# Q, K and V laid out by pairs of heads ahead of the kernel, and rows of decay stored once

## The chip, the cores and the metric

The kernel runs on one core of one Trainium2 chip. The metric is the time on the device in microseconds (us); three runs of the kernel before lay between 1041.75 and 1042.41 us, their median is 1041.98. Engines: TensorE (PE in the profile; PEld its weight loads), VectorE (DVE), ScalarE (ACT), GpSimd (POOL) and SyncE (SP), whose queue issues most transfers.

## The reference

Attention with a decay over 4 batches, 8 heads, 576 positions and 64 columns a head, then two feed-forward layers over 2304 tokens, 512 columns and 2048 inner columns.

```python
scores = scale * np.matmul(q, k.transpose(0, 1, 3, 2))
cum = np.cumsum(np.maximum(s, 0.0), axis=-1)
bias = -(cum[:, :, :, None] - cum[:, :, None, :])
scores = np.where(causal, -1000000000.0, scores + np.minimum(bias, 0.0))
attn = exp(scores - max) / (sum + 1e-09)        # by rows
x = (attn @ v), heads side by side               # 2304 x 512
x = leaky_relu(x @ w_in, 0.01) @ w_out           # first layer
out = softplus(x @ w_in2) @ w_out2               # second layer
```

## The kernel before

The 32 heads are worked off as 16 pairs: head 0 of a pair lies in partitions 0 to 63 of Q and K, head 1 in 64 to 127. A pair is cut into four units of query rows: tile 3 (512 keys), the last 64 rows of both heads together (128 rows), tile 2 (384 keys), and tiles 1 and 0 (256 and 128 keys). Q, K, V, BQ and BK have two buffers each, for even and odd pairs.

Scores of a unit (`Unit.scores`) are two products into one PSUM bank: Q by K in float32, and BQ by BK, which adds the decay. BQ and BK hold a few rows that are not zero: BK has the running sum of s in two parts (rows r and r+1, r = 0 or 64) beside ones in BQ, and BQ has its negative in two parts (rows r+32 and r+33) beside ones in BK. The two parts are a rounded float32r and its rest, since these products are float32r. `decay` scans s into c1 for all 32 heads, writes the four parts into bb, and bb is stored to DRAM (bb_d), from which `rows` fetches a pair's rows in five transfers; pair 0's rows go directly from bb.

Inputs come as they are, by position. `load` reads q and k of a pair into raw tiles (runs of 64 floats a position; in two transfers by head, and the last 64 positions in a third tile, rawl), and v into V. `prep` turns the raw tiles with nine TensorE transposes (line 251 four each for q and k, line 248 one for rawl) into PSUM, and one tick later copies them out: line 256 on ScalarE (Q), line 258 on VectorE (K), lines 260 and 263 on VectorE (the last positions: K and, for each head, Q).

The order of the work is written out by hand: a loop over units in which unit n+1 gets its scores, unit n its maxima (VectorE, line 316) and exponentials (ScalarE, line 330), unit n-1 its divisors and norms (GpSimd, line 341), and unit n-2 its transposes (line 358) and copies. Every engine runs its instructions in that order, so a step that waits holds up all that stands behind it on its engine. `pv` multiplies a pair's attention with V (line 389) one pair later. Each step of the loop may also issue one fill (12 matmuls of the first layer's first group, lines 141 and 586), from the second batch on and once the weights are split (lines 103 to 128). Weights come as 512 KB transfers on SP's queue. `prep(p + 1, ...)` stands at units 0 (q), 2 (last positions) and 1 (k) of pair p, `load(p + 2, ...)` directly behind each, `rows(p + 1)` behind q's at unit 0, `load(p + 1, "v")` at unit 3.

After the attention come the feed-forward layers, with weights streamed in and split on the way.

Of the kernel before, what the change touches and what calls it, by code (L numbers as in the profile page):

```python
# [30 lines left out]
def attn_moe_moe(ctx, tc, q, k, v, s, w1i, w1o, w2i, w2o, out):  # L31
    nc = tc.nc
    B, H, S, D = q.shape
    NT, DM = out.shape
# [21 lines left out]
    xl = keep.tile([P, KD, NT], F32R, tag="xl", name="xl")  # L56
    bb_d = dram.tile([B * H, 2, 2, S], F32R, tag="bb_d", name="bb_d")
    part = dram.tile([2 * B, P, KD, CW], F32, tag="part", name="part")
# [5 lines left out]
    def later(n, fn, *args):  # L64
        todo.setdefault(clock[0] + n, []).append((fn, args))
# [10 lines left out]
    def move(dst, src, queue=nc.sync):  # L76
        queue.dma_start(dst.bitcast(F32), src.bitcast(F32))
# [74 lines left out]
    def decay(cp, first):  # L152

        BH = B * H
        c0 = cp.tile([BH, S], F32, tag="c0", name="c0")
        c1 = cp.tile([BH, S], F32, tag="c1", name="c1")
        bb = cp.tile([BH, 2, 2, S], F32R, tag="bb", name="bb")
        one = bb[:, 0, 0, :].bitcast(F32)
        nc.sync.dma_start(c0, s.rearrange("b h s -> (b h) s"))
        first()  # L160
        nc.vector.memset(one, 1.0)

        nc.vector.tensor_scalar(c0, c0, 0.0, 1.0 / scale, op0=ALU.max, op1=ALU.mult)
        nc.vector.tensor_tensor_scan(c1, one, c0, 0.0, op0=ALU.mult, op1=ALU.add)
        nc.scalar.activation(bb[:, 1, 0, :], c1, AF.Copy)
        nc.scalar.activation(bb[:, 0, 0, :], c1, AF.Copy, scale=-1.0)
        hi = bb[:, 1, 0, :].bitcast(F32)
        nc.vector.tensor_tensor(bb[:, 1, 1, :], c1, hi, op=ALU.subtract)
        nc.vector.tensor_tensor(bb[:, 0, 1, :], hi, c1, op=ALU.subtract)
        return bb  # L170


    def attention(att, ps, fills):
        ident = att.tile([P, P], F32, tag="ident", name="ident")
        make_identity(nc, ident)

# [7 lines left out]
        V = two("V", [P, NB + 1, 2, D])  # L184
        raw = {nm: att.tile([P, NB, 2, D], F32, tag="raw" + nm, name="raw" + nm) for nm in "qk"}
        raw["l"] = att.tile([P, 2, D], F32, tag="rawl", name="rawl")
# [4 lines left out]
        def blank(i):  # L191
            bq, bk = BQ[i].bitcast(F32), BK[i].bitcast(F32)
            nc.gpsimd.memset(bq, 0.0)
            nc.gpsimd.memset(bk, 0.0)
            for j in range(2):
                for c in own[j]:
                    nc.gpsimd.memset(bq[j * D:j * D + 2, c], 1.0)
                nc.gpsimd.memset(bk[j * D + 32:j * D + 34], 1.0)
                nc.gpsimd.memset(Q[i][(1 - j) * D:(2 - j) * D, NB * P + j * TL:NB * P + (j + 1) * TL], 0.0)

        def zeros():
            for i in range(2):
                nc.gpsimd.memset(V[i][TL:, NB, :, :], 0.0)
# [6 lines left out]
        def load(p, nm):  # L210
            if p >= NP:
                return
            b, hs = heads(p)
            src = {"q": q, "k": k, "v": v}.get(nm)
            if nm == "l":
                for x, r in ((q, slice(0, TL)), (k, slice(TL, 2 * TL))):
                    nc.sync.dma_start(raw["l"][r], x[b, hs, NB * P:, :].rearrange("h p d -> p h d"))
                return
            t = V[p % 2] if nm == "v" else raw[nm]
            for j in range(2):  # L220
                nc.sync.dma_start(
                    t[:, :NB, j, :], src[b, hs.start + j, :NB * P, :].rearrange("(c p) d -> p c d", p=P)
                )
            if nm == "v":
                nc.sync.dma_start(t[:TL, NB, :, :], src[b, hs, NB * P:, :].rearrange("h p d -> p h d"))

        def rows(p, src, queue=(nc.sync, nc.sync)):

            if p < NP:
                b, hs = heads(p)  # L230
                for j in range(2):
                    h, r = b * H + hs.start + j, j * D
                    of = lambda e, c: src[h, e, :, c] if src is bb_d else src[h:h + 1, e, :, c]
                    n = 0
                    for c in own[j]:
                        m = n + c.stop - c.start
                        move(BQ[p % 2][r + 32:r + 34, c], of(0, slice(n, m)), queue[j])
                        n = m
                    move(BK[p % 2][r:r + 2], of(1, slice(0, S)), queue[j])

        def prep(p, nm):

            if p >= NP:
                return
            tag, bufs = ("a", 1) if p or nm == "q" else ("m", 1) if nm == "k" else ("t", 2)
            pm = ps.tile([P, 512], F32, tag=tag, name="pt_qk", bufs=bufs)
            if nm == "l":
                nc.tensor.transpose(pm[:, :P], raw[nm].rearrange("p h d -> p (h d)"), ident)
            else:
                for c in range(NB):  # L250
                    nc.tensor.transpose(pm[:, c * P:(c + 1) * P], raw[nm][:, c].rearrange("p h d -> p (h d)"), ident)  # L251

            def out():
                qt, kt = Q[p % 2], K[p % 2]
                if nm == "q" or nm == "k" and not p:
                    nc.scalar.activation((qt if nm == "q" else kt)[:, :NB * P], pm, AF.Copy)
                elif nm == "k":
                    nc.vector.tensor_copy(kt[:, :NB * P], pm)
                else:
                    nc.vector.tensor_copy(kt[:, NB * P:], pm[:, TL:2 * TL])  # L260
                    for j in range(2):
                        r = slice(j * D, (j + 1) * D)
                        nc.vector.tensor_copy(qt[r, NB * P + j * TL:NB * P + (j + 1) * TL], pm[r, :TL])

            later(1, out)


        class Unit:
# [11 lines left out]
            def scores(self):  # L280
                i = self.p % 2
                self.ps = [ps.tile([P, 512], F32, tag=f"s{j}", name="pt_s", bufs=2) for j in range(2)]
                if self.last:

                    for j, pt in enumerate(self.ps):
                        for x, y in ((Q[i], K[i]), (BQ[i], BK[i])):
                            nc.tensor.matmul(  # L287
                                pt[:, :self.W], x[:, NB * P:], y[:, j * self.W:(j + 1) * self.W],
                                start=x is Q[i], stop=x is BQ[i],
                            )  # L290
                    return

                for t, c in self.subs:
                    for x, y in ((Q[i], K[i]), (BQ[i], BK[i])):
                        for j in range(2):
                            r = slice(j * D, (j + 1) * D)
                            nc.tensor.matmul(  # L297
                                self.ps[j][:, c], x[r, t * P:(t + 1) * P], y[r, :(t + 1) * P],
                                start=x is Q[i], stop=x is BQ[i],
                            )  # L300
# [122 lines left out]
        def first():  # L423
            for nm in "qkl":
                load(0, nm)

        with pool("cum", side="right") as cp:
            bb = decay(cp, first)
            blank(0)
            for nm in "qkl":  # L430
                prep(0, nm)
                tick()
            tick()
            rows(0, bb, (nc.sync, nc.scalar))
            masks()
            zeros()
            blank(1)
            load(1, "q")
            load(0, "v")
            move(bb_d, bb)  # L440
            load(1, "k")
            load(1, "l")
        fill = fills()
# [10 lines left out]
        for n in range(len(units) + 3):  # L454
# [13 lines left out]
            if i == 0:  # L468
                prep(p + 1, "q")
                load(p + 2, "q")  # L470
                rows(p + 1, bb_d)
            elif i == 2:
                prep(p + 1, "l")
                load(p + 2, "l")
            tick()
# [8 lines left out]
            if u2:  # L484
                u2.evacuate(0)
                u2.transpose(1)
            if i == 1:
                prep(p + 1, "k")
                load(p + 2, "k")
            elif i == 3 and p + 1 < NP:  # L490
                load(p + 1, "v")
            elif i in (0, 2) and p:
                pv(p - 1, i == 0)
# [257 lines left out]


# [18 lines left out]
```

## Time and profile before

| | |
|---|---|
| median of three runs | 1041.98 us |
| profiled execution, whole | 1041.97 us |
| its span, first to last instruction | 1040.2 us |
| TensorE busy | 1009.9 us (97%), 5632 matmuls |
| VectorE, ScalarE, GpSimd busy | 512.5, 545.1, 581.3 us |
| moved by DMA | 61.20 MB in 89070 packets, 59616 of them under 512 B |
| granted clock | 0.995 |

The attention stage runs to about 280 us, and the feed-forward layers take the rest. Busy shares over the whole span say little of the stages; the stretches below do. Matmuls are pipelined, so the busy time of one reaches under the start of the next.

### The profile page before, as it was taken

To read this page: it belongs to the slowest core of one execution; us is meant where nothing else is said; L and a number is where in the kernel's file an instruction comes from. 1 tells how busy PE (TensorE), PEld (TensorE's weight loads), DVE (VectorE), ACT (ScalarE), POOL (GpSimd) and SP (SyncE) were. 2 spreads that over 40 slices of the span, in tenths; PEclk is the share of its full clock that TensorE was granted. 3 is DMA by queue.
4 is the path that set the end of the run, shared out by engine and by line. 5 is a ranking of instruction groups with operands and counts; after the bars stand their busy time and mean duration, and the time that the engine had idled before them with its cause. 6 is when DMAs were issued, how large, how long until landed. Compare 5 with 4: busy or idle time off the path is not lost.

```text
span 1040.2 us, 15671 instructions
## 1 busy us (share of the span) xinstructions
PE 1009.9 (97%) x5632; PEld 829.6 (80%) x5632; DVE 512.5 (49%) x1174; ACT 545.1 (52%) x1170; POOL 581.3 (56%) x592
## 2 busy tenths in 40 slices
PE   7899999999999999999999998999999999999998
PEld 4668788888898888888888886888777887788886
DVE  5886756555202222222232245645675677567443
ACT  4776767665436333333344354676556545564452
POOL 5765544543327433643456667666866676667453
PEclk9999999999999999999999999999999999999999
DMA  6433433231053101210121021001200121010202
GB/s 146 126 86 79 106 89 99 73 77 37 24 183 119 41 1 41 81 41 1 49 74 41 1 80 42 25 17 41 81 27 15 41 82 37 5 40 21 82 21 81
DMA packets 89070, 61.20 MB, mean 59 GB/s; under 512 B 59616, under 2 KB 82656, under 8 KB 88960
## 3 DMA queue, kind: packets, MB, share of 16 engines
q1 hardware_dynamic: 88980, 60.18, 19.6%
q8 instruction: 45, 0.74, 0.3%
q14 instruction: 33, 0.27, 0.1%
q10 hardware_dynamic: 12, 0.01, 0.0%
HBM read 51.60 MB, written 8.55 MB: 58 GB/s over the span
## 4 chain that ended last, share of the span: by engine, by line
PE 71%; POOL 10%; DVE 8%; issue 6%; ACT 4%; DVEq 0%; POOLq 0%; ACTq 0%
PE ps_h L141 29%; PE ps_out L698 26%; PE ps_o L586 4%; PE pt_v L389 4%; PE pt_s L297 3%; POOL t L666 3%; PE pt_t L358 3%; POOL gl L148 2%; POOL wm L118 2%; DVE wm L112 2%; PE pt_s L287 2%; ACT sc L330 1%; DVE wm L115 1%; DVE wm L109 1%; PE pt_qk L251 1%
## 5 line engine op out<-in xcount | busy, mean ns | idle before, releaser
L148 POOL TENSOR_TENSOR gl<-gf,gh 128x512 fp32r<-128x512 f32 (+2 forms) x148 | 177.8, 1202 | 238.3 <-ACT gh L147 230.9
L141 PE MATMUL ps_h<-xh,wih 128*128 128x512 f32 (+2 forms) x688 | 247.5, 360 | 1.0 <-ACT o L590 0.5
L141 PE MATMUL ps_h<-xl,wih 128*128 128x512 f32 (+2 forms) x688 | 245.6, 357 | 0.0
L141 PE MATMUL ps_h<-xh,wil 128*128 128x512 f32 (+2 forms) x688 | 244.5, 355 | 0.0
L341 POOL TENSOR_SCALAR sc<-sc,st 128x512 f32<-128x512 f32 (+4 forms) x160 | 87.7, 559 | 121.3 <-DVE st L337 38.9
L141 PEld LDWEIGHTS ps_h<-xh,wih 128*128 128x128 f32 x688 | 130.0, 189 | 21.6 <-ACT o L590 0.8
L141 PEld LDWEIGHTS ps_h<-xl,wih 128*128 128x128 f32 x688 | 130.0, 189 | 19.1
L141 PEld LDWEIGHTS ps_h<-xh,wil 128*128 128x128 f32 x688 | 129.9, 189 | 18.6
L709 DVE TENSOR_TENSOR acc<-ps_out,acc 128x512 f32<-128x512 f32 (+1 forms) x114 | 67.7, 655 | 128.0 <-PE ps_out L698 128.0
L147 ACT ACTIVATE gh<-gf 128x512 fp32r<-128x512 f32 (+2 forms) x148 | 85.3, 576 | 85.0 <-DVE gf L671 84.1
L652 ACT ACTIVATE gf<-ps_h 128x512 f32<-128x512 f32 (+2 forms) x68 | 36.6, 538 | 171.8 <-PE ps_h L141 171.8
L671 DVE TENSOR_TENSOR gf<-gf,t 128x512 f32<-128x512 f32 (+1 forms) x80 | 56.0, 700 | 133.6 <-POOL t L666 133.6
L109 DVE TENSOR_SCALAR wm<-wm 128x512 f32<-128x512 f32 x64 | 42.6, 666 | 156.3 <-ACT wm L103 147.7
L698 PE MATMUL ps_out<-woh,gh 128*128 128x512 f32 x288 | 115.1, 400 | 3.0 <-DVE acc L709 2.0
L698 PE MATMUL ps_out<-wol,gh 128*128 128x512 f32 x288 | 114.2, 397 | 0.0
L330 ACT ACTIVATE sc<-sc,st 128x512 f32<-128x512 f32 (+2 forms) x144 | 83.5, 582 | 56.9 <-DVE st L316 23.4
L118 POOL TENSOR_TENSOR wm<-wm,wt 128x512 int32<-128x512 int32 x64 | 88.0, 1376 | 28.2 <-DVE wm L115 28.2
L666 POOL TENSOR_TENSOR t<-e,t 128x512 f32<-128x512 f32 (+1 forms) x80 | 98.1, 1226 | 0.0
L698 PE MATMUL ps_out<-gh,woh 128*128 128x512 f32 (+2 forms) x272 | 97.1, 366 | 0.0
L698 PE MATMUL ps_out<-gh,wol 128*128 128x512 f32 (+2 forms) x272 | 96.8, 364 | 0.0
L698 PE MATMUL ps_out<-woh,gl 128*128 128x512 f32 x288 | 81.6, 401 | 5.5 <-POOL gl L148 5.5
L316 DVE CUSTOM_DVE_ANT_0 sc<-pt_s,mask 128x512 f32<-128x512 f32 (+2 forms) x144 | 66.5, 481 | 38.1 <-PE pt_t L358 24.2
(105 smaller groups left out, 1815.0 us busy)
## 6 DMA issues: line engine op xcount, KB each, us to landing
rawi<-in_moe_w_in SPq DMA_DIRECT2D x32, 512.0 KB
rawo<-in_moe_w_out SPq DMA_DIRECT2D x32, 512.0 KB
out<-acc SPq DMA_DIRECT2D x18, 256.0 KB
rawq<-in_q SPq DMA_DIRECT2D x32, 128.0 KB
rawk<-in_k SPq DMA_DIRECT2D x32, 128.0 KB
V<-in_v SPq DMA_DIRECT2D x32, 128.0 KB
part<-o SPq DMA_DIRECT2D x24, 144.0 KB
acc<-part SPq DMA_DIRECT2D x6, 576.0 KB
```

Of the source, the lines that this page charges most:

```text
L109: nc.vector.tensor_scalar(mf, mf, D_MIN, D_MAX, op0=ALU.max, op1=ALU.min)
L118: nc.gpsimd.tensor_tensor(m, m, t, op=ALU.add)
L141: nc.tensor.matmul(ps, a, b, start=n == 0, stop=n == 3 * KD - 1)
L147: nc.scalar.activation(gh, gf, AF.Copy)
L148: nc.gpsimd.tensor_tensor(gl, gf, gh.bitcast(F32), op=ALU.subtract)
L316: nc.vector.tensor_tensor_reduce(out=self.sc[:, j, c], in0=self.ps[j][:, c], in1=m, scale=-scale, scalar=3.0e38, op0=ALU.add, op1=ALU.min, ...
L330: nc.scalar.activation(x, x, AF.Exp, scale=-1.0, bias=self.stat(0, e), accum_out=self.stat(1, e))
L341: nc.gpsimd.tensor_scalar(x, x, self.stat(2, e), 1.0, op0=ALU.mult, op1=ALU.mult)
L666: nc.gpsimd.tensor_tensor(t, e, t, op=ALU.subtract)
L671: nc.vector.tensor_tensor(gf, gf, t, op=ALU.add)
L698: nc.tensor.matmul(ps, a, b, start=f == 0 and m == 0, stop=f == G - 1 and m == 2)
L709: nc.vector.tensor_tensor(d, o, d, op=ALU.add)
```

## The change

Ahead of the launch q, k and v are laid out anew (`lay_out`; values are only moved). For each pair, K is 128 x 576 and Q 128 x 640, already transposed, in the form that the tiles have (Q's last positions of both heads in columns of their own, with zeros in the other head's partitions), and V is 128 x 5 x 2 x 64 with zeros behind the last position. So a pair's q, k and v are one transfer each straight into Q, K and V. `prep`, the raw tiles, the transposes on TensorE and the copies out of PSUM are gone, and so are the memsets of V and of Q's corners.

Decay: BQ now holds the sum itself, beside -1 in BK, so bb has two parts a head and not four. BQ is blank with ones, where BK is zero. For pair 0, c1 itself goes into BK and BQ as float32, one row each, and the first pair's bias products are float32; `parts`, which splits c1 and stores bb_d, comes after the first rows, masks and v.

```diff
+        def blank(i, kq=(nc.gpsimd, nc.gpsimd)):
+            bq, bk = BQ[i].bitcast(F32), BK[i].bitcast(F32)
+            kq[0].memset(bk, 0.0)
+            kq[1].memset(bq, 1.0)
             for j in range(2):
+                r = j * D
+                kq[0].memset(bk[r + 32:r + 34], -1.0)
+                kq[1].memset(bq[r + 32:r + 34], 0.0)
+                kq[1].memset(bq[r:r + 2, NB * P + (1 - j) * TL:NB * P + (2 - j) * TL], 0.0)
...
+        def load(p, nm, queue=nc.sync):
+            if p < NP:
+                t, x = {"q": (Q, q), "k": (K, k), "v": (V, v)}[nm]
+                queue.dma_start(t[p % 2], x[p])
...
+                bq, bk = BQ[i], BK[i]
+                if not self.p:
+                    bq, bk = bq.bitcast(F32), bk.bitcast(F32)
...
         def first():
-            for nm in "qkl":
-                load(0, nm)
+            load(0, "k")
+            load(0, "q", nc.scalar)
+            blank(0, (nc.vector, nc.gpsimd))
 
         with pool("cum", side="right") as cp:
-            bb = decay(cp, first)
-            blank(0)
-            for nm in "qkl":
-                prep(0, nm)
-                tick()
-            tick()
-            rows(0, bb, (nc.sync, nc.scalar))
+            c1, parts = decay(cp, first)
+            rows(0, c1, (nc.sync, nc.scalar))
             masks()
+            make_identity(nc, ident)
             zeros()
+            load(0, "v")
+            parts()
             blank(1)
...
             if i == 0:
-                prep(p + 1, "q")
-                load(p + 2, "q")
+                load(p + 1, "q")
+                load(p + 1, "k")
                 rows(p + 1, bb_d)
-            elif i == 2:
-                prep(p + 1, "l")
-                load(p + 2, "l")
...
-            if i == 1:
-                prep(p + 1, "k")
-                load(p + 2, "k")
-            elif i == 3 and p + 1 < NP:
+            if i == 3 and p + 1 < NP:
                 load(p + 1, "v")
```

TensorE inside pair 1, before, from the transposes of the probabilities of pair 0's third unit on (pt_t; pt_qk is what the transposes of raw q and k write, pt_s are scores, pt_v products with V):

```order
L358 MATMUL pt_t<-ident,sc 128x128 x3
L251 MATMUL pt_qk<-ident,rawq 128x128 x4
L358 MATMUL pt_t<-ident,sc 128x128 x3
L389 MATMUL pt_v<-PA,V_95 64x192 x8
L389 MATMUL pt_v<-PZ,V_95 64x64 x2
L297 MATMUL pt_s<-K_90,Q_88 128x384 x2
L297 MATMUL pt_s<-BK_94,BQ_92 128x384 x2
L358 MATMUL pt_t<-ident,sc 128x128 x6
L251 MATMUL pt_qk<-ident,rawk 128x128 x4
```

The same place now:

```order
L323 MATMUL pt_t<-ident,sc 128x128 x6
L354 MATMUL pt_v<-PA,V_91 64x192 x8
L354 MATMUL pt_v<-PZ,V_91 64x64 x2
L262 MATMUL pt_s<-K_86,Q_84 128x384 x2
L262 MATMUL pt_s<-BK_90,BQ_88 128x384 x2
L323 MATMUL pt_t<-ident,sc 128x128 x6
L262 MATMUL pt_s<-K_86,Q_84 128x256 x2
L262 MATMUL pt_s<-BK_90,BQ_88 128x256 x2
```

Eight transposes have gone from between the probabilities' transposes, the value product and the scores; the ninth stood a few rows further on.

SP's queue before, from v of pair 1 to the last positions of pair 3; raw q and k are those of pair 3, the rows of decay those of pair 2:

```order
L221 DMA V_96<-in_v 128x4x64 x2
L225 DMA V_96<-in_v 64x2x64
L221 DMA rawq<-in_q 128x4x64 x2
L77 DMA BQ_91<-bb_d 2x576
L77 DMA BK_93<-bb_d 2x576
L77 DMA BQ_91<-bb_d 2x512
L77 DMA BQ_91<-bb_d 2x64
L77 DMA BK_93<-bb_d 2x576
L88 DMA rawi<-in_moe_w_in 128x4x256
L221 DMA rawk<-in_k 128x4x64 x2
L217 DMA rawl<-in_q 64x2x64
L217 DMA rawl<-in_k 64x2x64
```

The same place now:

```order
L212 DMA V_92<-in_v 128x640
L212 DMA Q_83<-in_q 128x640
L212 DMA K_85<-in_k 128x576
L79 DMA BK_89<-bb_d 2x576
L79 DMA BQ_87<-bb_d 2x576
L79 DMA BK_89<-bb_d 2x576
L79 DMA BQ_87<-bb_d 2x512
L79 DMA BQ_87<-bb_d 2x64
L90 DMA rawi<-in_moe_w_in 128x4x256
```

Q and K of pair 2 stand directly ahead of that pair's rows, where raw q of pair 3 stood, and the raw transfers behind the weights are gone.

ScalarE at the start, before (the DMAs are pair 0's rows of the second head):

```order
L46 ACT_TABLE_LOAD
L165 ACTIVATE bb<-c_109 32x576
L166 ACTIVATE bb<-c_109 32x576
L256 ACTIVATE Q_87<-pt_qk 128x512
L256 ACTIVATE K_89<-pt_qk 128x512
L77 DMA BQ_91<-bb 2x1x512
L77 DMA BQ_91<-bb 2x1x64
L77 DMA BK_93<-bb 2x1x576
L330 ACTIVATE sc,st<-sc,st 128x512
L256 ACTIVATE Q_88<-pt_qk 128x512
```

ScalarE at the start now:

```order
L48 ACT_TABLE_LOAD
L212 DMA Q_83<-in_q 128x640
L79 DMA BK_89<-c_102 1x16x36
L79 DMA BQ_87<-c_102 1x16x32
L79 DMA BQ_87<-c_102 1x16x4
L169 ACTIVATE bb<-c_102 32x576
L295 ACTIVATE sc,st<-sc,st 128x512 x2
```

The load of Q comes first; the rows no longer stand behind two splits and the copies of Q and K, and the copy of pair 1's Q between the exponentials is gone.

## Rows read from the trace of the kernel before

**Rows 1.** engines' busy us (instructions) by stretch: PE, PEld, DVE, ACT, POOL, clock, DMA, GB/s

```profile
13.00:78.00 65.00, 59.20 (x447) 42.05 (x445) 52.97 (x198) 47.47 (x130) 39.15 (x56) 1.00 0.49 122
78.00:95.00 17.00, 17.00 (x148) 14.76 (x144) 10.51 (x40) 10.65 (x31) 9.38 (x15) 1.00 0.35 86
95.00:121.00 26.00, 24.11 (x194) 18.06 (x192) 20.55 (x73) 19.31 (x54) 14.25 (x23) 1.00 0.35 85
121.00:280.00 159.00, 157.62 (x1289) 132.42 (x1290) 87.28 (x345) 99.64 (x282) 70.70 (x114) 1.00 0.27 71
```

**Rows 2.** groups by line, 0 to 300 us: count, busy us, mean ns, idle before

```profile
L251 PE MATMUL pt_qk<-ident,rawq 128*128 128x128 f32 x64 | 10.5, 292 | 4.8 <-DMA rawq<-in_q 4.8
...
L258 DVE COPY K<-pt_qk 128x512 f32<-128x512 f32 x15 | 10.3, 689 | 18.4 <-PE pt_qk L251 18.2
...
L263 DVE COPY Q<-pt_qk 64x64 f32<-64x64 f32 x32 | 6.9, 216 | 0.2
...
L260 DVE COPY K<-pt_qk 128x64 f32<-128x64 f32 x16 | 3.5, 217 | 1.1 <-PE pt_qk L248 1.0
...
L256 ACT ACTIVATE Q<-pt_qk 128x512 f32<-128x512 f32 x16 | 9.5, 594 | 5.6 <-PE pt_qk L251 5.6
```

**Rows 3.** order of time, TensorE, 181 to 187 us: start, us, line, operation, count

```profile
181.38 0.49 PE L358 MATMUL pt_t<-ident,sc 128*128 128x128 f32 x3
181.70 0.60 PE L251 MATMUL pt_qk<-ident,rawq 128*128 128x128 f32 x4
...
185.70 0.92 PE L297 MATMUL pt_s<-K,Q 64*128 64x384 f32 x4
186.16 0.63 PE L297 MATMUL pt_s<-BK,BQ 64*128 64x384 f32 x2
186.72 0.55 PE L358 MATMUL pt_t<-ident,sc 128*128 128x128 f32 x3
```

**Rows 4.** chain of waits, 26 to 77 us: start, us, what

```profile
31.29 0.60 DVE K L258
...
61.04 0.12 PE pt_qk L248
...
61.18 0.23 DVE K L260
...
61.78 0.14 issue
...
75.09 0.24 DVE Q L263
```

**Rows 5.** order of time, all engines, first 17 us

```profile
1.81 0.58 POOL L194 MEMSET BK<- 128x576 f32 x1
...
2.85 0.45 DVE L163 TENSOR_SCALAR c<-c 32x576 f32<-32x576 f32 x1 [1.41 <-DMA c<-in_s]
...
3.33 1.34 DVE L164 TENSOR_TENSOR_SCAN c<-bb,c 32x576 f32<-32x576 f32 x1
...
4.62 0.57 POOL L198 MEMSET BK<- 2x576 f32 x1
...
7.16 2.01 ACTq L77 DMA_DIRECT2D BQ<-bb  x2
...
9.27 0.58 ACTq L77 DMA_DIRECT2D BK<-bb  x1
...
11.76 0.76 PE L297 MATMUL pt_s<-BK,BQ 64*128 64x512 f32 x1 [1.24 <-POOL Q L199]
...
15.02 1.05 PE L251 MATMUL pt_qk<-ident,rawq 128*128 128x128 f32 x4
...
16.01 1.13 PE L297 MATMUL pt_s<-K,Q 64*128 64x384 f32 x4
```

**Rows 6.** order of time, SP's queue and TensorE, 40 to 50 us

```profile
40.03 0.92 SPq L221 DMA_DIRECT2D rawq<-in_q  x2
...
49.41 1.13 PE L297 MATMUL pt_s<-K,Q 64*128 64x512 f32 x4
```

More of the change, by code (lines that the diff above doesn't have):

```diff
@@ L32, in attn_moe_moe @@
     nc = tc.nc
-    B, H, S, D = q.shape
+    B, H, S = s.shape
+    D = v.shape[-1]
     NT, DM = out.shape
@@ L56, in attn_moe_moe @@
     xl = keep.tile([P, KD, NT], F32R, tag="xl", name="xl")
-    bb_d = dram.tile([B * H, 2, 2, S], F32R, tag="bb_d", name="bb_d")
+    bb_d = dram.tile([B * H, 2, S], F32R, tag="bb_d", name="bb_d")
     part = dram.tile([2 * B, P, KD, CW], F32, tag="part", name="part")
@@ L156, in decay, with parts @@
         c1 = cp.tile([BH, S], F32, tag="c1", name="c1")
-        bb = cp.tile([BH, 2, 2, S], F32R, tag="bb", name="bb")
-        one = bb[:, 0, 0, :].bitcast(F32)
+        bb = cp.tile([BH, 2, S], F32R, tag="bb", name="bb")
+        one = bb[:, 0, :].bitcast(F32)
         nc.sync.dma_start(c0, s.rearrange("b h s -> (b h) s"))
+        nc.vector.memset(one, 1.0)
         first()
-        nc.vector.memset(one, 1.0)
         nc.vector.tensor_scalar(c0, c0, 0.0, 1.0 / scale, op0=ALU.max, op1=ALU.mult)
         nc.vector.tensor_tensor_scan(c1, one, c0, 0.0, op0=ALU.mult, op1=ALU.add)
[L165 to L170, printed above, removed]
+        def parts():
+            nc.scalar.activation(bb[:, 0, :], c1, AF.Copy)
+            nc.vector.tensor_tensor(bb[:, 1, :], c1, bb[:, 0, :].bitcast(F32), op=ALU.subtract)
+            move(bb_d, bb)
+        return c1, parts
     def attention(att, ps, fills):
         ident = att.tile([P, P], F32, tag="ident", name="ident")
-        make_identity(nc, ident)
         ZQ = NB * P + 2 * TL
@@ L184, in attention @@
         V = two("V", [P, NB + 1, 2, D])
-        raw = {nm: att.tile([P, NB, 2, D], F32, tag="raw" + nm, name="raw" + nm) for nm in "qk"}
-        raw["l"] = att.tile([P, 2, D], F32, tag="rawl", name="rawl")
         PA = att.tile([P, 2, NB, P + TL], F32, tag="PA", name="PA")
@@ L190, in attention @@
         PB = att.tile([P, 2, NB - 1, 2 * P], F32, tag="PB", name="PB")
-        def blank(i):
+        def blank(i, kq=(nc.gpsimd, nc.gpsimd)):
             bq, bk = BQ[i].bitcast(F32), BK[i].bitcast(F32)
-            nc.gpsimd.memset(bq, 0.0)
-            nc.gpsimd.memset(bk, 0.0)
+            kq[0].memset(bk, 0.0)
+            kq[1].memset(bq, 1.0)
             for j in range(2):
[L196 to L199, printed above, removed]
+                r = j * D
+                kq[0].memset(bk[r + 32:r + 34], -1.0)
+                kq[1].memset(bq[r + 32:r + 34], 0.0)
+                kq[1].memset(bq[r:r + 2, NB * P + (1 - j) * TL:NB * P + (2 - j) * TL], 0.0)
         def zeros():
-            for i in range(2):
-                nc.gpsimd.memset(V[i][TL:, NB, :, :], 0.0)
             nc.gpsimd.memset(PZ[TL:], 0.0)
@@ L208, in heads, with rows @@
             return b, slice(2 * hp, 2 * hp + 2)
[L210 to L227, printed above, removed]
+        def load(p, nm, queue=nc.sync):
+            if p < NP:
+                t, x = {"q": (Q, q), "k": (K, k), "v": (V, v)}[nm]
+                queue.dma_start(t[p % 2], x[p])
+        def rows(p, src=bb_d, queue=(nc.sync, nc.sync)):
             if p < NP:
@@ L232, in rows @@
                     h, r = b * H + hs.start + j, j * D
-                    of = lambda e, c: src[h, e, :, c] if src is bb_d else src[h:h + 1, e, :, c]
+                    of = lambda c: src[h, :, c] if src is bb_d else src[h:h + 1, c]
+                    e = 2 if src is bb_d else 1
+                    move(BK[p % 2][r:r + e], of(slice(0, S)), queue[j])
                     n = 0
@@ L236, in rows @@
                         m = n + c.stop - c.start
-                        move(BQ[p % 2][r + 32:r + 34, c], of(0, slice(n, m)), queue[j])
+                        move(BQ[p % 2][r + 32:r + 32 + e, c], of(slice(n, m)), queue[j])
                         n = m
[L239 to L265, printed above, removed]
         class Unit:
@@ L285, in scores @@
                     for j, pt in enumerate(self.ps):
-                        for x, y in ((Q[i], K[i]), (BQ[i], BK[i])):
+                        for x, y in ((Q[i], K[i]), (bq, bk)):
                             nc.tensor.matmul(
                                 pt[:, :self.W], x[:, NB * P:], y[:, j * self.W:(j + 1) * self.W],
-                                start=x is Q[i], stop=x is BQ[i],
+                                start=x is Q[i], stop=x is bq,
                             )
@@ L293, in scores @@
                 for t, c in self.subs:
-                    for x, y in ((Q[i], K[i]), (BQ[i], BK[i])):
+                    for x, y in ((Q[i], K[i]), (bq, bk)):
                         for j in range(2):
@@ L298, in scores @@
                                 self.ps[j][:, c], x[r, t * P:(t + 1) * P], y[r, :(t + 1) * P],
-                                start=x is Q[i], stop=x is BQ[i],
+                                start=x is Q[i], stop=x is bq,
                             )
@@ L423, in first @@
         def first():
-            for nm in "qkl":
-                load(0, nm)
+            load(0, "k")
+            load(0, "q", nc.scalar)
+            blank(0, (nc.vector, nc.gpsimd))
         with pool("cum", side="right") as cp:
-            bb = decay(cp, first)
-            blank(0)
-            for nm in "qkl":
-                prep(0, nm)
-                tick()
-            tick()
-            rows(0, bb, (nc.sync, nc.scalar))
+            c1, parts = decay(cp, first)
+            rows(0, c1, (nc.sync, nc.scalar))
             masks()
+            make_identity(nc, ident)
             zeros()
+            load(0, "v")
+            parts()
             blank(1)
[L438 to L442, printed above, removed]
         fill = fills()
@@ L750, with lay_out @@
 _OUT = ((2304, 512), "float32")
+def lay_out(name, a):
+    import numpy as np
+    if name not in ("q", "k", "v"):
+        return np.ascontiguousarray(a)
+    B, H, S, D = a.shape
+    n, tl = S // P, S % P
+    a = a.reshape(B * H // 2, 2, S, D)
+    if name == "v":
+        r = np.zeros((B * H // 2, P, n + 1, 2, D), a.dtype)
+        r[:, :, :n] = a[:, :, :n * P].reshape(-1, 2, n, P, D).transpose(0, 3, 2, 1, 4)
+        r[:, :tl, n] = a[:, :, n * P:].transpose(0, 2, 1, 3)
+        return r
+    r = np.zeros((B * H // 2, 2, D, S + (tl if name == "q" else 0)), a.dtype)
+    r[..., :S] = a.transpose(0, 1, 3, 2)
+    if name == "q":
+        r[:, 1, :, S:] = r[:, 1, :, n * P:S]
+        r[:, 1, :, n * P:S] = 0
+    return r.reshape(-1, 2 * D, r.shape[-1])
 def kernel(**inputs):
@@ L760 @@
     for name in _INS:
-        a = np.ascontiguousarray(inputs[name])
+        a = lay_out(name, np.asarray(inputs[name]))
         if a.dtype == np.float64:
```

## The prediction

> **What bounds the kernel now.** I first read the stretches by engine [rows 1], then the groups by line [rows 2], then TensorE's and the chain's rows inside those stretches. The attention stage has two kinds of stretch. From 78 to 95 us and from 121 to 280 us TensorE is busy 17.00 of 17 and 157.62 of 159 us, because fill matmuls of the first feed-forward layer stand in every unit; VectorE is at 87.28 of 159 there. What leaves TensorE's queue there shortens the program. From 13 to 78 us (no fill yet) and from 95 to 121 us (the fill waits for weights) TensorE has gaps (59.20 of 65, 24.11 of 26) and VectorE is at 52.97 of 65 and 20.55 of 26. There the chain goes back and forth between VectorE, ScalarE and TensorE. Before 13 us everything waits for the first loads and the rows of decay. Behind 280 us the change leaves every instruction as it is.
>
> I call "a prep" what turns a pair's raw q and k into Q and K. There are 16: pairs 0 and 1 belong to the start, pairs 2 to 5 fall into 13 to 78 us, pair 6 into 78 to 95, pairs 7 and 8 into 95 to 121, pairs 9 to 15 into 121 to 280. So 6 preps lie in stretches led by the chain, 8 in stretches led by TensorE.
>
> **What the change takes out.** A prep has nine 128x128 transposes on TensorE, one 128x512 copy of Q on ScalarE (0.59 us), one 128x512 copy of K (0.69) and three short ones (0.22 each) on VectorE [rows 2]. That is 0.59 us of ScalarE and 1.34 to 1.35 us of VectorE a pair.
>
> *Where TensorE leads.* The page gives the transposes 10.5 us for 64, 0.164 each [rows 2]. That is a matmul's busy time with its tail, under which the next one already runs. What one takes from the queue is the distance between starts: three transposes of L358 start at 181.38 us and the next group at 181.70 [rows 3], 0.32 for three, 0.107 each. Nine are 0.96 us, and 8 preps are 7.7 us. The other end is the page's 0.164, 1.48 a prep and 11.8 us in all. I take 0.107, since in a full queue the start distance is what the successor feels.
>
> *Where the chain leads.* In 26 to 77 us, which holds the preps of pairs 2 to 5, 18 pieces of the chain are prep work (transposes of raw q or l, copies of Q and K). They run from the copy of K at 31.29 us to the copy of Q at 75.09 and sum to 3.94 us, 0.99 a prep; behind some stands a short wait, 0.14 us as at 61.78 [rows 4]. I take 1.1 a prep. The ends: nothing, if a parallel chain of nearly equal length takes over, and 1.94, if all the copies' time (1.35 and 0.59) comes off. 6 preps x 1.1 = 6.6 us (0 to 11.6).
>
> *The start.* Scores of the first unit need the rows of decay. Before, the scan of s starts at 3.33 us and takes 1.34, then two splits and the copies of Q and K follow, and ScalarE issues its three row DMAs from 7.16 us on, the last at 9.27; the matmul that needs that one starts at 11.76, 2.49 later [rows 5]. Now the rows leave c1 directly. VectorE has three memsets ahead of it that GpSimd did before: 0.58 for a whole tile as L194 and 0.57 each for two strips as L198, 1.72 in all, against an idle 1.41 us before L163 [rows 5]. So the scan ends 0.31 us later, at 4.98, and the row DMAs start at 4.98 where 7.16 stood: 2.2 us earlier. Then the transposes of raw q that separate the second unit's scores from the third's, 15.02 to 16.01 [rows 5], are gone: 1.0 us. Start: 3.2 us. Both ends: 1.0 us if the rows are again late, since q and k are whole transfers ahead of them; 5 us if the exponentials, which stand behind the copy of Q on ScalarE, move up by more than the matmuls.
>
> *The first pair's bias in float32.* Sixteen bias matmuls of pair 0 become float32 ones. The rows show both kinds at one shape: the float32 scores have four records for two 64x384 products, span 0.92, and are followed after 0.46; the bias has two records, span 0.63, and is followed after 0.56 [rows 3]. By the distance between starts float32 costs nothing; by the spans 0.29 a step. Pair 0 has 3136 bias columns against 768 in this step, 4.08 times as many, so 0 to 1.2 us. I take 0, the start distance again.
> The Trainium skill ("FP8 and Floating Point Precision", TensorE Precision Notes) says that true FP32 takes four passes through the array. The trace shows two records a product and no four times longer step, so it agrees with part of that at most; by the rule the sum would be some microseconds smaller (third rival).
>
> *At nothing.* Loads of q, k and v become one transfer each, with longer runs; rows of decay to the queries are stored once instead of twice; the float32 split of c1, its copy and bb_d now come behind the first rows, with nothing waiting before pair 1. Memsets of V fall away on GpSimd, whose idle time covers them. On SP's queue a pair's q and k now stand directly ahead of its rows, one pair ahead instead of two. Cover for that: the place in the queue ahead of the rows of pair 3 is at 40.03 us, and the scores of pair 3 start at 49.41 [rows 6], 9.4 us later. Q and K are 128x640 and 128x576 floats, 0.62 MB, 5.1 us at the 122 GB/s of 13 to 78 us [rows 1], and 2.5 us from issue to use [rows 5]: 7.6 us, 1.8 to spare. If this cover goes, TensorE waits at each pair's first score (fourth rival).
>
> **Sum.** 7.7 + 6.6 + 3.2 = 17.5 us. The profiled execution took 1041.97 us (span 1040.2 and 1.77 around it), the median of the runs is 1041.98, so no correction: 1024.5 us.
>
> **Rivals.**
> 1. *More comes off*: transposes cost their busy time and all the copies' time leaves the chain. 11.8 + 6 x 1.94 + 4.5 for the start = 27.9: 1014 us. For it: VectorE near 0.82 of 13 to 78 us. Against it: start distances of 0.107, and only 18 of the chain's pieces are prep work.
> 2. *The chain's stretches give nothing*: weight splits and softmax keep the same period, since GpSimd's and ScalarE's waits there don't depend on Q and K. 7.7 + 3.2: 1031 us. For it: many chains of like length; against it: copies stand in VectorE's queue in front of the softmax work, whichever chain leads.
> 3. *Float32 bias costs twice the float32 scores' span*: (1.84 - 0.63) x 4.08 = 4.9 us on the start: 1029.4 us. For it only the page's rule; against it the two records.
> 4. *Late loads, slower*: the pair's q and k, now asked for one pair ahead and sharing the DMA engines with 512 KB weight loads and v, arrive behind the point where TensorE wants them, at the first score of each of 14 pairs. It turns the sign from 17.5 / 14 = 1.25 us of waiting a pair on. If another 0.5 MB is in flight, 4.2 us at 122 GB/s less the 1.8 to spare make 2.4 us a pair, 34 us: 1058 us. Against it: longer runs should move faster, and weight loads stand in only some of the pairs.
> 5. *It does nothing*, because TensorE's work is hidden in the chain and the chain's in TensorE: 1042 us. The full queue of 121 to 280 us speaks against it.
>
> **How the numbers follow.** Forecast 0.68, rival 1 0.12, rival 2 0.10, rival 3 0.04, rivals 4 and 5 0.03 each. The forecast's own range is 1019 to 1029; with rivals 1 to 3 the range is 1015 to 1031, which leaves out rivals 4 and 5 and the far side of rival 1. About 0.2% (2 us) is what a measurement here tells from no change: faster 0.94, same 0.03, slower 0.03.
>
> **What would show it.** The second bias matmul of pair 0 starts near 9.6 us; the third unit's scores near 12.8; a filled pair takes about 1 us less (from the value matmuls of one pair to those of the next); an unfilled one 1.1 us less; the feed-forward layers start about 17.5 us earlier and take the same time. Waits of TensorE for a DMA at each pair's first scores would make it wrong, and so would filled pairs that shorten by 1.5 us.

## The result, and the profile after

The changed kernel took 1024.72 us (median of four, 1024.32 to 1025.01) against 1042.20 us beside it; the ratio is 0.983 with a 95% interval of 0.982 to 0.985. 1024.5 us were forecast. The profiled execution took 1025.01 us with a span of 1023.0, 17.2 us below the 1040.2 before. Of the runs below, one execution in ten of the kernel with the decay alone took 1240.39 us at a granted clock of 0.754; its ratio leaves that one out.

The same stretches of the kernel after, cut where the same work stands (columns as in [rows 1]):

```profile
13.00:75.00 62.00, 55.09 (x427) 38.59 (x426) 50.45 (x183) 46.51 (x130) 39.62 (x56) 1.00 0.41 129
75.00:92.00 17.00, 17.00 (x141) 14.20 (x139) 9.27 (x37) 11.93 (x33) 10.74 (x16) 1.00 0.28 83
92.00:116.00 24.00, 23.04 (x188) 16.51 (x187) 19.40 (x75) 18.86 (x56) 17.15 (x25) 1.00 0.34 107
116.00:262.00 146.00, 145.27 (x1187) 121.55 (x1185) 76.40 (x299) 91.84 (x260) 66.54 (x108) 1.00 0.24 77
```

As in [rows 1], the second and fourth are filled by TensorE, the first and third are not. The work of a filled stretch simply got shorter. In the others TensorE's waits for the copies of Q (2.4 us from 27 to 121 us before) are gone, and those for ScalarE's copy PB of the probabilities have grown from 2.2 to 4.8 us (24 to 116 us after).

TensorE at the place of [rows 3], order of time, kernel after:

```profile
168.01 0.49 PE L323 MATMUL pt_t<-ident,sc 128*128 128x128 f32 x3
168.25 0.38 PE L143 MATMUL ps_h<-xh,wih 128*128 128x288 f32 x1
```

Three transposes of probabilities, and 0.24 us later the fill begins; in [rows 3] four transposes of raw q stood between.

How long a pair takes is read from the first value product of one pair to that of the next. Pair 10, before:

```profile
184.14 1.52 PE L389 MATMUL pt_v<-PA,V 128*64 128x192 f32 x16
...
202.26 1.52 PE L389 MATMUL pt_v<-PA,V 128*64 128x192 f32 x16
```

and after:

```profile
170.34 1.52 PE L354 MATMUL pt_v<-PA,V 128*64 128x192 f32 x16
...
187.48 1.52 PE L354 MATMUL pt_v<-PA,V 128*64 128x192 f32 x16
```

18.12 us have become 17.14. Read so over the whole program (us, profiled executions; the two columns on the right are experiments below, in which first the transposes and then also the copies are put back):

| stretch | preps in it | before | after | transposes back | copies too |
|---|---|---|---|---|---|
| start to pair 0's first value product | 0, 1 | 27.11 | 24.01 | 25.60 | 26.39 |
| pairs 0 to 4 | 2 to 5 | 57.27 | 54.05 | 54.63 | 57.33 |
| pairs 4 to 5 | 6 | 16.95 | 15.61 | 16.53 | 16.97 |
| pairs 5 to 7 | 7, 8 | 29.48 | 26.76 | 27.35 | 29.49 |
| pairs 7 to 14 | 9 to 15 | 124.14 | 117.19 | 123.59 | 124.12 |
| pairs 14 to 15 | none | 15.70 | 15.70 | 15.70 | 15.70 |
| from there to the end | none | 769.51 | 769.65 | 769.76 | 769.74 |

The pair without a prep is unchanged to the hundredth, and what follows it to 0.14 us. So 3.10 us came from the start and 14.23 from 14 preps: 8.29 in the filled stretches (rows three and five) and 5.94 in the others (rows two and four).

The start, order of time, kernel after:

```profile
3.51 0.76 DVE L165 TENSOR_SCALAR c<-c 32x576 f32<-32x576 f32 x1
...
4.31 1.35 DVE L166 TENSOR_TENSOR_SCAN c<-bb,c 32x576 f32<-32x576 f32 x1
...
5.68 0.61 ACTq L79 DMA_DIRECT2D BK<-c  x1
...
6.34 1.23 ACTq L79 DMA_DIRECT2D BQ<-c  x2
...
8.51 2.32 PE L262 MATMUL pt_s<-BK,BQ 64*128 64x512 f32 x4 [1.73 <-DMA BQ<-c]
...
10.76 1.33 PE L252 MATMUL pt_s<-K,Q 128*128 128x288 f32 x2
...
11.88 1.17 PE L252 MATMUL pt_s<-BK,BQ 128*128 128x288 f32 x2
...
12.15 0.71 ACT L295 ACTIVATE sc<-sc,st 128x512 f32<-128x512 f32 x1
...
13.80 1.12 PE L252 MATMUL pt_s<-BK,BQ 128*128 128x288 f32 x2
...
14.85 0.92 PE L262 MATMUL pt_s<-K,Q 64*128 64x384 f32 x4
...
16.24 0.60 PE L262 MATMUL pt_s<-K,Q 64*128 64x256 f32 x4
```

Against [rows 5]: the row DMAs on ScalarE begin at 5.68 and not 7.16, the first bias product at 8.51, the third unit's scores at 14.85 and not 16.01. The second unit (10.76 to 14.85) takes 4.09 us.

Differences at the start need care. There all matmuls take about twice as long as later, and where that ends differs from execution to execution. The changed kernel was profiled a second time (the first of the last three runs below), order of time:

```profile
10.75 1.33 PE L252 MATMUL pt_s<-K,Q 128*128 128x288 f32 x2
...
13.63 0.65 PE L252 MATMUL pt_s<-BK,BQ 128*128 128x288 f32 x2
...
14.21 0.92 PE L262 MATMUL pt_s<-K,Q 64*128 64x384 f32 x4
```

The second unit begins at the same time, but its last product takes 0.65 us and not 1.12, and pair 0's first value product starts at 23.38 us and not 24.01. In both executions TensorE is without a gap from 8.5 us on. A trace also holds a list of changes of the granted clock, which no view prints; its first entry, a rise to 1.00, stands at 14.74 us in the first execution and at 13.46 in the second, where the doubling ends. Before its first entry the list says nothing, and the 1.00 that the views print there is no reading. So an end that came 1.28 us earlier was worth 0.63 us, half of it, with nothing else changed. The first entry stands at 16.48 us in the kernel before. By the same half, 0.87 us of the start's 3.10 go with the earlier end, an estimate; whether the change brought that or the execution, no run shows.

### The profile page after: what moved, and what is told of

It reads as the page before. It is cut to its first block, busy times and chain, and to the rows that moved or that the text cites. A ratio compares the mean times of both kernels' runs of the same rounds, so it can differ in the third digit from the quotient of the medians.

```text
span 1023.0 us, 15109 instructions
## 1 busy us (share of the span) xinstructions
PE 992.6 (97%) x5498; PEld 812.5 (79%) x5498; DVE 499.3 (49%) x1113; ACT 536.4 (52%) x1152; POOL 581.3 (57%) x585
## 4 chain that ended last, share of the span: by engine, by line
PE 74%; POOL 9%; DVE 7%; issue 5%; ACT 3%; DMA 1%; SPq 0%; DVEq 0%; POOLq 0%; ACTq 0%
PE ps_h L143 30%; PE ps_out L651 28%; PE pt_v L354 4%; PE ps_o L539 4%; PE pt_s L262 4%; PE pt_t L323 3%; POOL t L619 3%; POOL gl L150 2%; POOL wm L120 2%; PE pt_s L252 2%; DVE wm L114 2%; ACT sc L295 1%; DVE wm L111 1%; DVE wm L117 1%; POOL wil L130 1%
```

## The experiments

Each was compared with the kernel before on its own chip, where that took 1041.69 to 1042.10 us.

**The decay alone.** The kernel before with the new `decay`, `blank`, `rows` and float32 for pair 0, and with raw tiles, transposes and copies as they were.

```diff
-            bb = decay(cp, first)
-            blank(0)
+            c1, parts = decay(cp, first)
+            rows(0, c1, (nc.sync, nc.scalar))
             for nm in "qkl":
                 prep(0, nm)
                 tick()
             tick()
-            rows(0, bb, (nc.sync, nc.scalar))
```

> The decay half of the change alone: raw q, k and v, the transposes and the copies stay as in the kernel before. Theory A (the prediction): rows of decay leave earlier and float32 bias costs nothing, so the start gains about 2 us: 1040 us. Theory C (read from the trace after): pair 0's bias in float32 takes 3 to 4 us more of TensorE than in float32r and eats what the earlier rows give: 1041 to 1044 us, no gain.

1041.81 us, ratio 0.9998 (0.9988 to 1.0007): no gain, as theory C had it. Rows leave early and the third unit is no earlier, order of time:

```profile
5.37 0.62 ACTq L77 DMA_DIRECT2D BK<-c  x1
...
10.58 1.92 PE L305 MATMUL pt_s<-BK,BQ 64*128 64x512 f32 x4
...
16.08 0.92 PE L305 MATMUL pt_s<-K,Q 64*128 64x384 f32 x4
```

Pair 0's first value product starts at 27.66 us, 0.55 later than before, although the clock's first entry stands earlier here (14.64 us against 16.48).

**The layout alone.** The changed kernel with the old decay: four parts, split first, and float32r for pair 0.

```diff
-            c1, parts = decay(cp, first)
-            rows(0, c1, (nc.sync, nc.scalar))
+            bb = decay(cp, first)
+            blank(0)
+            rows(0, bb, (nc.sync, nc.scalar))
```

> The layout half alone: inputs by pairs, no transposes, no copies, but four parts of decay, split before pair 0's rows leave, and pair 0's bias in float32r. Theory A: the steady pairs are as short as after the change (17.1 us where filled) and the start is 2 us later than after: 1027 us. Theory C: the start loses 2 us of earlier rows and wins 3 to 4 us of float32r: 1022.5 to 1024 us.

1026.17 us (1025.18 to 1028.16; ratio 0.985, 0.984 to 0.987). The median is nearer to theory A's 1027, but it does not decide between the two, as the clock below shows. Its pairs are those of the changed kernel (53.95, 15.61, 26.75, 117.21). Its start, order of time:

```profile
7.58 1.80 ACTq L79 DMA_DIRECT2D BQ<-bb  x2
...
12.19 0.76 PE L254 MATMUL pt_s<-BK,BQ 64*128 64x512 f32 x1 [1.15 <-DMA BK<-bb]
...
15.58 1.65 PE L254 MATMUL pt_s<-K,Q 64*128 64x384 f32 x4
```

The rows leave no earlier than before the change (7.58 us), and yet the first value product starts at 24.69, 2.42 us earlier than before. So most of what the start gains comes from the preps of pairs 0 and 1 that are gone. The decay half adds 0.68 us to that in the profiles and 1.45 by the medians. Neither is a price for it: the clock's first entry stands at 17.43 us here and at 14.74 in the changed kernel, by the half above 1.3 us (an estimate), more than the 0.68. What the decay half is worth stays open.

**Transposes put back.** Nine a pair, in the old places, out of K into the bank of the value products; nobody reads the result.

```diff
+            pm = ps.tile([P, 512], F32, tag="a", name="pt_qk", bufs=1)
+            for c in range(1 if nm == "l" else NB):
+                nc.tensor.transpose(pm[:, c * P:(c + 1) * P], kt[:, c * P:(c + 1) * P], ident)
```

> The changed kernel with nine transposes a pair put back on TensorE in their old places (they read K of the running pair, into the bank that the value products use; nobody reads the result, no copies). Theory A (a transpose costs its distance between starts, 0.107 us): a filled pair grows from 17.14 to 18.1 us; in all 8 filled ones 7.7 us plus some 3 us elsewhere: 1034 to 1037 us. Rival B (it costs its busy time, 0.164 us): a filled pair grows to 18.6 us: 1038 to 1042 us.

1034.57 us. Pair 10 again, order of time:

```profile
176.91 1.52 PE L364 MATMUL pt_v<-PA,V 128*64 128x192 f32 x16
...
195.04 1.52 PE L364 MATMUL pt_v<-PA,V 128*64 128x192 f32 x16
```

18.13 us: theory A's price. Over the 8 filled preps it is 7.32 us, 0.92 each (0.96 by 0.107 a transpose; the page's 0.164 would be 1.48). The trace's busy time of a matmul was not its price. At the start, where one prep is put back (pair 1's), the first value product comes 1.59 us later.

**Copies too.** The same with the copies out of the bank, into tiles that nobody reads.

```diff
+                if nm == "q":
+                    nc.scalar.activation(Qs[:, :NB * P], pm, AF.Copy)
+                elif nm == "k":
+                    nc.vector.tensor_copy(Ks[:, :NB * P], pm)
+                else:
+                    nc.vector.tensor_copy(Ks[:, NB * P:], pm[:, TL:2 * TL])
+                    for j in range(2):
+                        r = slice(j * D, (j + 1) * D)
+                        nc.vector.tensor_copy(Qs[r, NB * P + j * TL:NB * P + (j + 1) * TL], pm[r, :TL])
```

> As the run with the transposes put back, and with the copies as well (Q on ScalarE, K and the three short ones on VectorE, into tiles that nobody reads). Theory A: filled pairs as with the transposes alone (18.1 us), unfilled pairs some 0.5 us longer than with the transposes alone, since copies are on the chain there: 1038 to 1040 us, so that these two together are the whole of the steady pairs' gain. Rival: copies are covered everywhere, same time as with the transposes alone (within 1 us).

1041.69 us (the kernel before on the same chip: 1042.10), above the range: the gain is given back, and stretch by stretch the pairs are those before, within 0.1 us (the table). The loads by pairs stay in this kernel, so they carry none of the pairs' gain. The rival fell: in unfilled stretches copies cost 4.84 us (2.70 and 2.14, 0.81 a prep) and transposes 1.17, in filled ones copies 0.97 and transposes 7.32. The forecast was low because unfilled pairs lose 0.8 and not 0.5 us by the copies, the filled ones 0.97 in all and not nothing, and the start 0.79 more.

**Pair 0's bias in float32r**, from the same float32 rows (the low part of the decay is left out in pair 0).

```diff
-                if not self.p:
-                    bq, bk = bq.bitcast(F32), bk.bitcast(F32)
```

> The changed kernel with pair 0's bias products in float32r from the same float32 rows (one row a head, so the low part of the decay is left out in pair 0). Nothing else differs. Theory A (by distances between starts float32 costs nothing): no change, 1024.7 us. Theory C (four passes against one): the second unit's four products take 1.5 us less and the start about 3 us less in all: 1021 to 1022.5 us.

1022.42 us, theory C. Order of time:

```profile
5.68 0.62 ACTq L79 DMA_DIRECT2D BK<-c  x1
...
8.15 1.11 PE L260 MATMUL pt_s<-BK,BQ 64*128 64x512 f32 x2 [1.45 <-POOL BQ L195]
...
9.18 1.33 PE L250 MATMUL pt_s<-K,Q 128*128 128x288 f32 x2
...
10.24 0.58 PE L250 MATMUL pt_s<-BK,BQ 128*128 128x288 f32 x1
...
11.95 1.65 PE L260 MATMUL pt_s<-K,Q 64*128 64x384 f32 x4
```

The rows leave at the same 5.68 us. The second unit takes 9.18 to 11.95, 2.77 us and not 4.09, with one record a bias product and not two; the third unit starts 2.90 us earlier, and the first value product at 21.48 and not 24.01. The clock's first entry stands at nearly the same time (14.66 and 14.74 us), so these two profiles can be compared: 2.53 us, of which 0.36 is an earlier first bias product. By the medians, each against the kernel before on its own chip, the gain is 19.55 us here and 17.48 and 17.63 in the two series of the changed kernel. So float32 cost 1.9 to 2.5 us.

**BK of pair 0 blanked by GpSimd.**

```diff
-            blank(0, (nc.vector, nc.gpsimd))
+            blank(0)
```

> The changed kernel with BK of pair 0 blanked by GpSimd and not by VectorE ahead of the scan. Theory: the scan, which ended at 5.66 us, ends 0.9 us earlier, and pair 0's rows, which left at 5.68 us, leave at about 4.8: 1024 us. Rival: masks on GpSimd come 1.7 us later (they ended at 6.0 us) and bias rows have to wait for GpSimd's memsets instead: no change, 1024.7 us or a little more.

1023.52 us. The row DMAs leave at 5.06, 0.62 us earlier; GpSimd's masks were not what held up the start. The direction is the theory's, the medians differ by less than the runs spread (1023.01 to 1024.65). The profile does not settle the size, as the clock's first entry stands at 11.70 us in it.

**Pair 0's rows from the two parts**, bias in float32r and exact as in the other pairs.

```diff
-                if not self.p:
-                    bq, bk = bq.bitcast(F32), bk.bitcast(F32)
...
-            c1, parts = decay(cp, first)
-            rows(0, c1, (nc.sync, nc.scalar))
+            bb, parts = decay(cp, first)
+            parts()
+            rows(0, bb, (nc.sync, nc.scalar))
```

> The changed kernel with pair 0's rows taken from the two parts after the split, so that its bias is float32r and exact as in all other pairs; the rows leave one copy and one subtraction later (about 1.5 us). Theory A: 1.5 us slower, 1026 us. Theory C: 1.5 us later rows against 3 us or more of float32 passes: 1022.5 to 1024 us.

1023.52 us (1022.75 to 1023.90). The rows leave at 7.24 us, 1.56 later than after the change, and the first value product (22.75) is still 1.26 and 0.63 us earlier than in the two profiles of the changed kernel. The float32 passes cost more than the split on the rows' way.

**Loads two units later.**

```diff
             if i == 0:
-                load(p + 1, "q")
-                load(p + 1, "k")
                 rows(p + 1, bb_d)
+            elif i == 2:
+                load(p + 1, "q")
+                load(p + 1, "k")
```

> The changed kernel with the loads of the next pair's q and k two units later (unit 2 in place of unit 0), which takes away about 7 of the 9 us of cover. Theory A (7.6 us from issue to use): TensorE waits 3 to 5 us at the first scores of most pairs: 1060 to 1090 us. Rival: the transfers take 4 us or less, so that only unfilled pairs wait a little: 1025 to 1035 us.

1024.88 us (1024.42 to 1028.28), the changed kernel's time: both theories missed. SP's queue isn't tied to the step in which an instruction stands; it runs ahead until something makes it wait. Pair 3's load of Q and its first scores, order of time, after the change:

```profile
32.40 0.43 SPq L212 DMA_DIRECT2D Q<-in_q  x1
...
44.75 1.13 PE L262 MATMUL pt_s<-K,Q 64*128 64x512 f32 x4
```

and with the loads two units later:

```profile
37.55 0.50 SPq L212 DMA_DIRECT2D Q<-in_q  x1
...
47.83 1.13 PE L262 MATMUL pt_s<-K,Q 64*128 64x512 f32 x4
```

12.35 us of cover became 10.28, not 5. Of pairs 1 to 15 only pair 1 waited in the profiled execution (K asked for at 14.01 us behind a 512 KB load):

```profile
20.83 2.08 PE L262 MATMUL pt_s<-K,Q 64*128 64x512 f32 x4 [2.87 <-DMA K<-in_k]
```

That execution is the longest of the four, 1028.28 us against 1024.42 to 1024.96. From 20.0 us on, inside this wait, its granted clock is 0.50 for 6.8 us, and its first value product comes at 27.56 and not 24.01. So a single late load is the fourth rival in small. Otherwise the edit did not take the cover away, so it says little of the rival.

**Loads behind v.** So q and k were put where the queue must wait: behind v at the end of unit 2, whose transfer waits for the value products of the pair before.

```diff
             if i == 0:
-                load(p + 1, "q")
-                load(p + 1, "k")
                 rows(p + 1, bb_d)
...
-            if i == 3 and p + 1 < NP:
-                load(p + 1, "v")
-            elif i in (0, 2) and p:
+            if i in (0, 2) and p:
                 pv(p - 1, i == 0)
+            if i == 2 and p + 1 < NP:
+                for nm in "vqk":
+                    load(p + 1, nm)
```

> The changed kernel with the next pair's q and k asked for behind its v, and v at the end of unit 2, where its transfer waits for the value products of the pair before: now SP's queue can't run ahead, and the scores of the next pair follow at once on TensorE. It prices the fourth rival. Theory: issue to use takes 5 to 7 us, TensorE waits most of it at each of 15 pairs: 1085 to 1120 us. Rival: transfers are fast (3 us): 1050 to 1070 us.

1125.27 us (one run), above both ranges. The waits of TensorE for K (us, times, longest):

```profile
PE pt_s L262 <- DMA K<-in_k: 78.7, 16, 6.3
```

One of them, order of time:

```profile
74.80 0.43 SPq L212 DMA_DIRECT2D Q<-in_q  x1
75.27 0.42 SPq L212 DMA_DIRECT2D K<-in_k  x1
...
79.44 2.08 PE L262 MATMUL pt_s<-K,Q 64*128 64x512 f32 x4 [5.09 <-DMA K<-in_k]
```

4.17 us from the issue of K to its use, 4.64 from that of Q, for three transfers of 0.95 MB in all. 74.0 us of waits (without pair 0's 4.7) are 4.9 a pair. The other 27 us of the 101 go with slower matmuls, as I read it: the same scores that took 1.13 us take 2.08 behind the wait. Stretches around this wait (columns as in [rows 1]; the eighth number is the granted clock):

```profile
76.00:80.00 4.00, 0.56 (x2) 0.53 (x4) 0.53 (x4) 1.61 (x7) 0.27 (x1) 0.72 0.93 334
80.00:84.00 4.00, 4.00 (x14) 2.16 (x11) 0.97 (x2) 0.00 (x0) 0.00 (x0) 0.50 0.04 13
```

During the wait the clock falls to 0.50, the lower of its two levels, and stays there behind it. So a queue that must wait costs 101 us here, three times the 34 us that I gave the fourth rival. The changed kernel's queue runs ahead, and TensorE does not wait for K once after pair 0's first scores.

**Both edits of the start, and the copy on VectorE.** Three kernels on one chip (the third is shown against the second): the changed one again, one with the two parts and GpSimd's memsets, one that also copies the upper part on VectorE.

```diff
-            nc.scalar.activation(bb[:, 0, :], c1, AF.Copy)
+            nc.vector.tensor_copy(bb[:, 0, :], c1)
```

> The changed kernel again, on the same chip as the next two, as their measure: 1024 to 1025.5 us.

1024.06 us (1023.71 to 1024.57).

> The changed kernel with both edits that helped the start: pair 0's rows from the two parts, with its bias in float32r, and BK of pair 0 blanked by GpSimd. Theory C (the rows' way and the passes of float32 add): 1.2 us of the two parts and 0.7 to 1.2 of the memsets: 1022 to 1023 us. Rival: the second edit is covered, since masks on GpSimd are then what the first maxima wait for: 1023.5 us.

1023.29 us (1022.19 to 1024.12), the rival's number; the second edit shows no gain over the two parts alone.

> As the run with both edits, and the upper part of c1 is copied by VectorE and not by ScalarE, so that the split needs no change of engine: rows some 0.3 us earlier, 1022 to 1022.7 us. Rival: no difference that can be measured.

1022.79 us (1022.47 to 1023.53), which doesn't overlap with the changed kernel's runs. Its bias is exact, and it has the lowest median of the exact kernels here: 0.982 of the kernel before (0.981 to 0.983). It is not told apart from the other two with the two parts, whose runs overlap with its own. Its start, order of time:

```profile
3.22 0.45 DVE L165 TENSOR_SCALAR c<-c 32x576 f32<-32x576 f32 x1 [1.78 <-DMA c<-in_s]
3.31 0.88 POOL L197 MEMSET BK<- 2x576 f32 x1
3.70 1.34 DVE L166 TENSOR_TENSOR_SCAN c<-bb,c 32x576 f32<-32x576 f32 x1
...
5.08 1.05 DVE L169 CAST bb<-c 32x576 fp32r<-32x576 f32 x1
...
7.01 1.18 ACTq L79 DMA_DIRECT2D BK<-bb  x1
```

The copy takes 1.05 us on VectorE, and the rows leave at 7.01 us. From the kernel with both edits, which differs in this copy alone, the medians differ by 0.5 us, less than those runs spread; the comparison between the two is open. The profiles do not settle it: the third unit's scores start at 13.44 us here and at 13.69 in the kernel with both edits, the first value products at 21.88 and 23.39, and the clock's first entry stands at 13.56 against 16.75.

## Why the prediction was right, and where it was not

**Filled stretches** (forecast 7.7 us): 8.29. Transposes made 7.32 of it, at the start distance that I took; 0.97 were the copies, which I had put at nothing there. Single pairs shortened by 0.54 to 1.47 us, most of them by 0.98 to 1.01.

**Unfilled stretches** (6.6): 5.94, 0.99 a prep against 1.1. It was read from the chain as prep work of 0.99 a prep plus short waits; the waits did not count. Its make-up was right: copies on VectorE and ScalarE carried it, transposes only 1.17 us. The gain was uneven: 0.80 a prep for pairs 2 to 5, 1.36 for pairs 7 and 8.

**The start** (3.2): 3.10, but by luck: errors cancelled. The step "by the distance between starts float32 costs nothing" failed: it cost 1.9 to 2.5 us (pair 0's bias in float32r against float32), above the 0 to 1.2 that I allowed it. In [rows 3] the distance from the scores to the bias (0.46) and from the bias to the next group (0.56) do not price each product: what fits is that a record of float32 starts before the array is done with those ahead, so that the later group pays. Only the sum of both, against the same sum with float32 bias, prices it. At the shape of [rows 3] that is 1.39 us after the change (14.85 to 16.24) against 1.02 (185.70 to 186.72): 0.37 a step, which by the prediction's 4.08 makes 1.5 us, an estimate. For the second unit, in the stretch in which matmuls took twice as long as later, it is the changed kernel's 4.09 us against 2.77 in float32r. (Pair 0 has ten bias products, not the sixteen of the prediction; its sum goes by the columns, which are right.) The Trainium skill's rule that I weighed there ("FP8 and Floating Point Precision", TensorE Precision Notes: four passes for true FP32) agrees with this trace: two records a product, and 1.32 us more for the second unit's two products of 288 columns, 0.66 each. By the rule, three more passes of 288 columns at 1.2 GHz, the clock's lower level, would be 0.72 us a product, an estimate. The third rival had the mechanism right with 4.9 us as its price, about twice the measured one.

What made up for it: I counted 1.0 us for the preps of pairs 0 and 1 that leave the start, and the layout alone brought 2.42 with no earlier rows; pair 1's prep alone, put back, took 2.38 (1.59 and 0.79). ScalarE's second exponential shows it. Before, it stood behind the copy of pair 1's Q, order of time:

```profile
16.11 0.60 ACT L256 ACTIVATE Q<-pt_qk 128x512 f32<-128x512 f32 x1 [3.88 <-PE pt_qk L251]
16.61 0.71 ACT L330 ACTIVATE sc<-sc,st 128x512 f32<-128x512 f32 x1
```

After the change it starts at 12.15 us, and with the copies put back at 15.42. The earlier end of the doubled times, estimated at 0.87 us above, made up for some of it too; no term of the prediction held it. The rows left 1.5 us earlier and not 2.2, since the scan ended at 5.66 and not 4.98: the memsets on VectorE were not followed at once by the next instruction, and L165 took 0.76 us where L163 had taken 0.45. So the sign "the third unit's scores near 12.8" did not come: they start at 14.85 and, in the second profile, at 14.21.

**At nothing**: right. What follows the last pair's first value product, the feed-forward layers above all, took 769.65 against 769.51 us, and SP's queue never held TensorE up after pair 0. The cover of 9.4 us that I read was not the real one, since the queue runs ahead of the loop: pair 3 had 12.35 us, so there was more to spare than 1.8.

**Rivals.** The first fell with the start distance, the second and fifth with the table. The third was right in mechanism, and its price was covered at the start by what came off there. The fourth needs a queue that waits.

## What to carry to other kernels

In a full TensorE queue, price an instruction by the distance between starts over a whole sequence that holds it, never by its busy time, and never by one distance between two unlike matmuls. A removed step pays where its stretch is led: the same prep was worth 0.92 us as transposes in one stretch and 0.81 us as copies in another. Before a microsecond of difference at the start is put down to an edit, look in both traces for where the doubled matmul times end. A load's cover is set by what its queue waits for, and not by the step of the loop in which it is written.

## What the hardware showed that I had not expected

VectorE and GpSimd seem to hold each other up at the start. The same VectorE instruction beside the same GpSimd memset, order of time, in the kernel with both edits:

```profile
3.26 0.94 DVE L165 TENSOR_SCALAR c<-c 32x576 f32<-32x576 f32 x1 [1.81 <-DMA c<-in_s]
3.31 0.57 POOL L197 MEMSET BK<- 2x576 f32 x1
```

In the kernel with the copy on VectorE (its first two rows above) it is 0.45 and 0.88 us: once the one, once the other is longer by some 0.3 to 0.5 us. The Trainium skill ("GPSIMD Engine Reference", Specifications) names SBUF interfaces that the two share, with contention for VectorE instructions in a 2-port mode or with two SBUF inputs; that it is the cause here no run shows.

Near the start, a float32 product of 288 columns (two of its records) takes 1.17 us where it takes 0.65 later, and the views print a granted clock of 1.00 throughout. The list of clock changes explains the print: it has no entry before the end of the doubling, which it puts at 11.70 to 17.43 us in the profiles here. What sets the moment stays open; the two profiles of one and the same kernel differ by 1.28 us, and the three kernels with the two parts, whose first bias products start within 0.22 us of each other, by 3.19 (13.56, 15.48 and 16.75 us). Behind the 5 us waits of the run with loads behind v the same doubling comes with an entry, a granted clock of 0.50.
